# A hand-ordered fused attention and expert kernel: all 766 steps in another order, with engines and buffers assigned anew

## The chip, the cores and the metric

The kernel runs on one core of one Trainium2 chip. The metric is device microseconds (us) of one execution. A core has five engines that run their own instruction streams in order: TensorE (PE in the profile, with its weight loads shown apart as PEld), VectorE (DVE), ScalarE (ACT), GpSimd (POOL) and SyncE (SP). Data moves by DMA, issued here from SyncE, GpSimd and ScalarE. Times are the median of three runs; beside them stands one execution taken by the profiler.

## The reference

Two layers are computed one after the other, for a batch of 4, 8 heads, 768 positions and a head width of 64. The first is sparse attention: each position attends to the keys less than 16 positions away, and to 24 block summaries (the maximum of the keys and the mean of the values over each block of 32). The second is causal attention by four experts of width 64 with top-2 gating on its output.

```python
k_sum = k.reshape(B, H, nb, block, D).max(axis=3)
v_sum = v.reshape(B, H, nb, block, D).mean(axis=3)
...
scores_all = np.concatenate([scores_l_m, scores_s], axis=-1)
...
return np.matmul(a, v_all).astype(np.float32)
...
for e in range(E):
    q = x @ wq[e]
    k = x @ wk[e]
    v = x @ wv[e]
    ...
    ye = a @ v @ wo[e]
```

## The kernel before, in words

The work is cut into 766 steps. A step is a small function that issues one to 48 instructions on one engine, for example "transpose the keys of one pair of heads" or "copy one PSUM result to SBUF". `make_plan` builds the list of steps: for each it gives a name, the engines that may run it, the buffers that it reads and writes, and, for TensorE steps, a mode. The mode tells how the step uses the array: 0 is the whole 128x128 array, 1 is row tiles of 64 (64 rows by 128 columns), 2 is column tiles (64 or 32 columns). Where two successive TensorE steps have different modes, the array changes its shape.

Nothing in the program decides the order at run time. `TABLE` is the order, written out: each entry is the step's index in the plan, a letter for its engine (P TensorE, V VectorE, A ScalarE, G GpSimd, S SyncE) and the slots of the buffers that first come into use in it. `emit` walks the table and issues each step in that order. So the table fixes three things: the order of each engine's own queue, which engine runs a step that several could run, and which physical buffer (slot) a value takes. A step waits, through semaphores, for the steps that write what it reads and for those that last used its slot. The number of slots of each buffer class stands in `SLOTS` (PSUM itself has eight banks).

The names carry the batch b, the pair of heads c (four to a batch) and sometimes a half u or a column group cc. They are used below as follows.

- Startup: `id16`, `idr`, `mt`, `sel`, `pi` build constants; `vone0` to `vone5` write the ones column of the six `vb` slots; `knz`, `kwz`, `vtz`, `v2o`, `zz`, `w1m` clear or fill buffers; `at` is a dummy exponential.
- Loads: `dk` and `dq` bring keys and queries (line 261 and line 266, from GpSimd); `dv` brings the values of one pair (lines 284 to 287, from SyncE); `dvs` brings values for the block sums (line 339); `dw` and `dwv` bring weights (lines 501 and 507).
- Sparse attention, for each pair: `hc` copies the window edges inside the value buffer; `bs` (line 304), `be` and `ds` make the block means of the values by matmul for the first two batches, and `tr` (line 347) by a tree of additions for the others; `tk` and `tq` transpose keys and queries (line 366); `kw`, `rk`, `ksc`, `cq` move the transposed keys, their block maxima and the queries to SBUF; `sc` makes the scores (lines 414 and 420), `ex` the exponential (line 427), `av` the product with the values (line 437); `rc` and `xm` normalise, `tx` transposes (line 463), `hi` and `lo` split the result into two half-precision parts.
- Experts, for each batch: `vp` (lines 554 and 557) makes values and gate logits, `lg`, `v2`, `ga`, `gx`, `gb`, `gc` the gating; `pp` (line 630) makes queries and keys of two experts, `pc` moves them; `sp` (line 654) makes scores, `es` (line 662) the exponential, `dm` (line 667) the causal mask; `aw` (line 678) the product with the values; `r2`, `wv`, `tw`, `ct` scale and transpose; `op` (line 737), `oc` and `od` make, move and store the output.
- `fl` are filler matmuls (line 769), which compute nothing that is used; an `fl` given to ScalarE issues nothing.

Lines 168 and 170 are the helper `copy`: a copy or cast on ScalarE has line 168, one on VectorE or GpSimd has line 170.

Steps of two batches are interleaved: the experts of batch b run among the sparse attention of batch b+1. The last batch's experts run alone.

Of the kernel before, what the change touches and what calls it, by code (L numbers as in the profile page):

```python
# [15 lines left out]
S = 768  # L16
# [43 lines left out]
62,G, 122,P,4.2.2 236,S,4 100,V, 105,P,5.1.1 101,V, 82,P,2.1.1 148,G, 106,A, 81,P, 124,V, 102,P,0.0.0 83,V, 123,A,  # L60
125,G, 107,V, 109,P,6.0 233,G,2 103,A, 84,V, 45,G, 130,P,4.4 144,S,0 110,A, 104,V, 143,S, 269,P,7.0.0 131,A, 141,S,
235,G, 128,P,2.5 271,V, 63,P,6.1 129,A, 145,S,1 108,G, 133,P,0.0.2 270,A, 64,V, 140,S, 132,P, 142,S, 252,P,4.2.2
134,V, 111,P,2.0 135,V, 242,G,0 65,G, 254,V, 113,P,6.1 112,A, 237,G, 85,P,0.1.1 114,A, 86,V, 136,P,2.2.2 272,G, 137,A,
115,P,6.1.0 273,P,5.1 138,V, 150,G, 116,P, 274,A, 87,V, 46,V, 253,A, 238,P,2.0 117,V, 118,V, 246,S,5 277,P,0.2 239,V,
275,P,4.3 278,A, 119,P,6.3.3 256,P,3.2 276,A, 120,V, 241,G, 286,P,2.1.1 303,P,0.0.0 257,A, 194,P,4.0 121,V, 406,S,0
304,A, 244,S,2 255,G, 288,V, 149,G, 196,P,6.1 195,A, 305,V, 240,G, 287,A, 260,P,4.4 147,V, 407,S, 280,P,0.0.1 261,A,
409,S, 247,G, 290,P,3.0 197,A, 307,P,2.1 291,V, 279,P, 308,A, 204,P,4.0 402,S,4 281,V, 213,P,6 152,P,2.0.0 205,A,
282,V, 214,A, 245,G, 258,P,0.5 154,V, 283,P,4.4.4 259,A, 153,V, 408,S, 198,P,6 215,G, 201,P,2 284,V, 146,S, 199,A,
289,G, 248,P,0.1 418,S,0 306,G, 285,V, 401,G,1 202,A, 309,P,6.0 249,V, 210,P,4 310,A, 262,P,2.1.2 211,A, 263,P, 251,G,
165,P,0.2 250,A, 404,S,3 264,V, 265,V, 415,G,0 294,P,6.1 403,G, 166,A, 266,P,4.5.5 292,P,2.2 295,A, 267,V, 158,P,0  # L70
293,A, 400,G,0 151,A, 155,P,6 410,G, 159,V, 268,V, 160,A, 311,P,2.3 157,V, 207,P,4 312,A, 167,P,0.0 156,V, 161,V,6.0
208,A, 163,V, 411,G,0 314,P,2.0.0 162,A, 168,V, 432,P,7.2 313,P, 164,V, 433,A, 169,P,4.1 315,V, 172,P,0 170,A, 316,V,
413,G, 296,P,6.1.1 584,S,0 582,S, 585,S, 449,P,2.0 583,S, 173,A, 181,P,4 203,G, 450,V, 297,P, 412,G, 182,A, 184,P,0
178,P,2 416,S,2 298,V, 299,V, 185,A, 175,P,4 179,A, 209,G, 317,P,0.6.6 183,G, 300,P,6.7.7 174,G, 318,V, 176,A, 206,G,
428,P,2.2.2 200,G, 445,P,3.1.1 171,G, 319,V, 301,A, 177,G, 362,P,4.1 429,A, 414,G,2 447,V, 186,G, 180,G, 302,V,
364,P,0.0 448,A, 576,G,1 446,A, 430,V, 212,G, 586,G, 217,P,0.0.6 363,A, 218,P, 365,V, 431,A, 216,P, 375,P,2.0 219,V,
369,P,4 376,A, 187,P,1.1.0 220,V, 189,P, 587,G,1 370,A, 188,P, 434,P,2.5 190,V, 366,P,6 191,V, 323,P,4.1.1 367,A,
435,A, 436,P,0.4 417,G, 325,V, 420,S,0 453,P,6.3 423,S, 192,P,2.0 324,V, 454,A, 421,S, 320,P,4 193,V, 422,S, 368,G,
437,A, 578,S,5 405,G, 221,P,2.1 322,A, 372,P,6 222,V, 479,P,0.0.0 373,A, 419,G, 462,P,1.2.1 321,V, 381,P,2 223,P,4.0
464,V, 480,A, 577,G,2 335,P,6.2 382,A, 224,V, 463,A, 377,G, 383,G, 590,G,2 326,P,2 336,A, 481,V, 225,S, 371,G, 374,G,  # L80
378,P,4 327,V, 333,P,6.0 328,A, 329,V,1.1 424,G, 331,V, 330,A, 379,A, 229,P,2.2 332,V, 334,A, 451,P,4.0 230,V, 380,G,
226,P,0.4 452,A, 425,G,0 346,P,6.1 227,V, 343,P,4 347,A, 385,P,1.0.2 384,P, 386,P, 344,A, 228,S, 349,P,0 387,V,
604,P,6.1.2 350,A, 599,S,0 345,G, 388,V, 337,P,4 597,S, 427,G, 466,P,7.1 338,A, 606,V, 340,P,0 456,P,2.0.2 341,A,
605,V, 348,G, 455,P, 465,G, 467,A, 482,G, 483,P,4.2 457,V, 438,P,0.1.0 607,G, 458,V, 484,A, 588,G, 439,P, 389,P,6.0
580,S,4 440,V, 352,P,4 468,P,2.2 390,V, 353,A, 351,G, 469,A, 470,P,4.1 441,V, 354,G, 487,P,6.3 339,G, 471,A, 342,G,
621,P,2.2.1 625,P,3.0 591,G,1 488,A, 622,V, 608,P,0.1 594,S,3 579,G, 485,P,4.0 609,A, 355,P,0.1.6 623,V, 356,P, 626,A,
357,P, 426,G, 486,A, 459,P,0.0.0 358,V, 442,P,2.1.1 359,V, 460,A, 489,P,4.0.1 624,G, 443,A, 581,G, 461,V, 490,P,
473,P,6.1.2 444,V, 592,S,0 612,P,0.5 589,G, 491,V, 360,P,2.1 492,V, 613,A, 472,P, 361,V, 493,P,4.2.2 474,V, 629,P,0.4
598,S, 475,V, 494,A, 596,S, 394,P,2.0 630,A, 495,V, 391,P,6.4 395,A, 476,P,0.3.3 392,A, 396,S, 610,P,4.0 477,V,
627,P,2.3 611,A, 393,S, 538,P,6.1 478,V, 231,S, 628,A, 540,P,4.0 539,A, 600,G, 397,P,0.0 541,V, 642,P,2.2 398,A,  # L90
# [12 lines left out]
573,P,4.0 683,V, 706,G, 20,A,3 682,A, 571,A, 724,G, 707,P,1.0.0 684,V, 708,P, 22,A,3 574,A, 572,S, 734,P,6 710,V,
# [798 lines left out]
```

## Time and profile before

| what | us |
|---|---|
| median of 3 runs | 162.57 |
| lowest and highest of them | 161.71, 163.44 |
| the profiled execution's own time | 163.03 |
| its span, from the first to the last instruction | 161.3 |
| TensorE busy in it | 146.8 |
| ScalarE busy | 117.9 |
| VectorE busy | 116.6 |
| GpSimd busy | 111.8 |

The profiled execution is 0.46 us above the median of the runs. The 1.7 us between its span and its own time lie outside the program's instructions. The granted TensorE clock is 1.0 in all stretches. A busy time is the union of an engine's instructions; TensorE's matmuls overlap each other, so its busy share says that it had work, not how fast it went. A row of the timeline gives start, duration, engine, line, operation, output and inputs, shape and count, and in brackets how long the engine had been idle before it and who ended that.

### The profile page before, as it was taken

The page shows a single profiled execution, that of the slowest core. Times are in us where ns is not written, and L with a number is a line of the kernel's source. Part 1 is how long each engine was busy: PE and PEld are TensorE (multiplying, and loading weights), DVE is VectorE, ACT ScalarE, POOL GpSimd, SP SyncE. Part 2 cuts the span into 40 slices and gives each one's busy share as a digit, 9 for nine tenths or more (in the row PEclk, how much of TensorE's full clock was granted, in tenths as well). Part 3 has the DMA queues.
Part 4 walks back from the last instruction along what each step waited for, and adds up shares of the span by engine and source line. Part 5 has one row for each costly group of instructions (what it writes and reads, how often), then busy time and mean ns, then how long its engine had stood idle before and what let it go on. Part 6 is the DMA issues. An engine that isn't in the chain of part 4 may idle for free.

```text
span 161.3 us, 6957 instructions
## 1 busy us (share of the span) xinstructions
PE 146.8 (91%) x2999; PEld 108.0 (67%) x2999; DVE 116.6 (72%) x241; ACT 117.9 (73%) x150; POOL 111.8 (69%) x181
## 2 busy tenths in 40 slices
PE   0249998899999999999999999999999998999997
PEld 0127796786776866688656979666778895476742
DVE  5675488989885577986877887847978578247770
ACT  3032499758998969988978795787867894999540
POOL 6899969777775999969999999629994340135100
DMA  3999999998699995993899749886000000030746
GB/s 27 210 220 212 205 179 227 209 219 163 154 176 207 228 207 135 171 201 53 201 219 221 216 107 161 191 291 254 24 0 4 4 4 0 6 130 0 257 167 230
DMA packets 44158, 24.57 MB, mean 152 GB/s; under 512 B 33120, under 2 KB 40544, under 8 KB 43744
## 3 DMA queue, kind: packets, MB, share of 16 engines
q1 hardware_dynamic: 35280, 16.52, 43.2%
q0 software_dynamic: 7488, 6.29, 26.2%
q10 hardware_dynamic: 1360, 1.32, 2.3%
q8 instruction: 23, 0.38, 1.0%
q14 instruction: 7, 0.06, 0.1%
HBM read 24.13 MB, written 6.29 MB: 189 GB/s over the span
## 4 chain that ended last, share of the span: by engine, by line
PE 65%; POOL 21%; issue 6%; ACT 4%; DVE 3%; POOLq 0%; DVEq 0%; ACTq 0%
PE ps L437 12%; PE ps L630 11%; POOL vb L170 7%; PE ps L554 6%; PE ps L678 6%; PE ps L304 4%; PE ps L366 4%; PE ps L654 4%; PE ps L737 3%; PE ps L463 3%; PE ps L414 3%; POOL vt L347 3%; PE ps L769 3%; POOL a L667 2%; PE ps L420 2%
## 5 line engine op out<-in xcount | busy, mean ns | idle before, releaser
L662 ACT ACTIVATE a<-ps 128x1024 f16<-128x1024 f32 (+1 forms) x48 | 41.8, 918 | 5.2 <-PE ps L654 4.8
L667 POOL TENSOR_SCALAR_AFFINE_SELECT a<-a 128x256 f16<-128x256 f16 x48 | 18.6, 406 | 21.0 <-ACT a L662 20.4
L427 ACT ACTIVATE aT<-ps 120x768 f32<-120x768 f32 x32 | 25.0, 816 | 9.2 <-PE ps L420 9.0
L437 PE MATMUL ps<-vb,aT 120*64 120x65 f32 x768 | 27.3, 224 | 1.2 <-issue 0.6
L437 PEld LDWEIGHTS ps<-vb,aT 120*64 120x64 f32 x768 | 24.4, 138 | 4.3 <-issue 2.1
L170 POOL COPY vb<-vb 32x1408 f32<-32x1408 f32 x16 | 21.9, 1373 | 2.9 <-DMA vb<-in_v_dram 2.1
L630 PE MATMUL ps<-hi,wqk 128*128 128x384 f16 x128 | 23.1, 326 | 0.7 <-ACT ob L168 0.3
L347 POOL TENSOR_TENSOR vt<-vt 120x1024 f32<-120x1024 f32 (+3 forms) x16 | 19.2, 1200 | 6.4 <-issue 4.1
L630 PEld LDWEIGHTS <-wqk 128*128 128x128 f16 x128 | 11.8, 98 | 9.6 <-issue 2.2
L382 DVE TENSOR_REDUCE ks<-ps 128x24 f16<-128x768 f16 x16 | 15.1, 951 | 3.7 <-PE ps L366 3.3
L482 DVE TENSOR_TENSOR lo<-ps,hi 128x768 f16<-128x768 f32 x16 | 15.1, 954 | 1.3 <-ACT hi L168 1.1
L452 DVE TENSOR_TENSOR x<-ps,rec 128x768 f32<-128x768 f32 x16 | 15.3, 956 | 0.5
L366 PE MATMUL ps<-idr,kn 100*64 100x100 f16 x256 | 8.5, 218 | 7.3 <-DMA kn<-in_k_dram 7.3
L654 PE MATMUL ps<-qk,qk 64*128 64x512 f16 (+3 forms) x128 | 14.4, 306 | 0.5 <-ACT qk L168 0.4
L554 PE MATMUL ps<-wvg,hi 128*128 128x264 f16 x96 | 13.8, 275 | 0.1
L170 POOL COPY vb<-vu 24x768 f32<-24x768 f32 x16 | 13.2, 822 | 0.8
L168 ACT COPY kw<-ps 128x1152 f16<-128x1152 f16 x12 | 13.5, 1133 | 0.0
L168 ACT COPY qT<-ps 128x768 f16<-128x768 f16 x12 | 9.5, 806 | 5.3 <-PE ps L366 5.2
L678 PE MATMUL ps<-v,a 128*128 128x65 f16 x336 | 12.3, 193 | 0.2
L366 PEld LDWEIGHTS <-kn 100*64 100x64 f16 x256 | 7.0, 116 | 8.1 <-DVE vb L210 5.7
L678 PEld LDWEIGHTS <-a 128*128 128x128 f16 x336 | 11.0, 97 | 2.1 <-issue 1.0
L737 PE MATMUL ps<-wo,wT 128*128 128x512 f16 (+1 forms) x50 | 11.9, 371 | 0.0
(95 smaller groups left out, 273.8 us busy)
## 6 DMA issues: line engine op xcount, KB each, us to landing
vb<-in_v_dram SPq DMA_DIRECT2D x32, 176.0 KB, 6.1
out_dram<-ob SPq DMA_DIRECT2D x9, 512.0 KB, 3.4
vt<-in_v_dram SPq DMA_DIRECT2D x16, 192.0 KB
kn<-in_k_dram POOLq DMA_DIRECT2D x6, 384.0 KB, 7.5
qn<-in_q_dram POOLq DMA_DIRECT2D x6, 384.0 KB, 7.4
out_dram<-ob ACTq DMA_DIRECT2D x2, 512.0 KB
kn<-in_k_dram POOLq DMA_DIRECT2D x4, 192.0 KB, 5.5
qn<-in_q_dram POOLq DMA_DIRECT2D x4, 192.0 KB, 5.5
```

The costliest lines, as they stand in the source:

```text
L168: nc.scalar.copy(dst, src)
L170: en(e).tensor_copy(dst, src)
L347: en(e).tensor_tensor(y[0:120], x[0:120, 0:w], x[0:120, w:2 * w], AL.add)
L366: nc.tensor.transpose(dst[64 * hp:64 * hp + 64, p * s:p * s + p], src[:, hh + hp, 64 * s:64 * s + 64], idt)
L427: nc.scalar.activation(T["aT"][aT.slot][0:KR], pbank(sc, 2)[0:KR, :, 0:384], AF.Exp, scale=SCALE)
L437: nc.tensor.matmul(pbank(av, 2)[o:o + 64, u, 65 * (2 * (t // 2) + hp):65 * (2 * (t // 2) + hp) + 65], a[0:KR, hp, 64 * t:64 * t + 64], T[" ...
L554: nc.tensor.matmul(p[:, i, 0:264], hi_(ch)[:, cols], T["wvg"][:, ch, :], start=(ch == 0), stop=False, skip_group_check=True)
L630: nc.tensor.matmul(pbank(pp, 2)[:, u, 0:384], T["wqk"][:, cc, ch, j, :], hi_(ch)[:, 384 * u:384 * u + 384], start=(ch == 0), stop=(ch == N ...
L654: nc.tensor.matmul(pbank(sp, 2)[:, ep, c0:c0 + w], T["qk"][qk[1].slot][r, 128 * tj:128 * tj + 128], T["qk"][qk[0].slot][r, n0:n0 + w], sta ...
L662: nc.scalar.activation(a2v(u), pbank(sp, 2)[:, :, 0:ln], AF.Exp, scale=SCALE / (XS * XS))
L667: nc.gpsimd.affine_select(m, m, [[0, 2], [1, 128]], AL.is_ge, 0.0, base=0, channel_multiplier=-1)
L678: nc.tensor.matmul(pbank(av, 2)[:, ep, 65 * ti:65 * ti + 65], a2v(u)[:, ep, o:o + 128], T["v2"][v2.slot][:, tj, 2 * cc + ep, :], start=(tj ...
```

## The change

Only `TABLE` changes: every step is there once, as before, and the functions of the steps and the buffer sizes are the same. The order of each engine's queue, the engine of 61 steps and the slots are new. The order before has 111 changes of array shape between successive TensorE steps, the new one 121. The coarse order is the same (batches and stages follow each other as before); most steps move by a few places.

Among the steps that change engine are: `ds00`, `ds01` and `hc01` from GpSimd to ScalarE, `ds03` and `ds12` from ScalarE to GpSimd; `ksc` five from GpSimd to ScalarE and two the other way; `kw` four from ScalarE to VectorE and one the other way; `cq`, `hi`, `pc`, `v2`, `oc` and `ct` some in each direction; `cvg` from VectorE to ScalarE; eight `fl`.

The first four lines and the last ones, as they were and as they become (the lines between are of the same kind; what the prediction speaks of is given by names below):

```diff
 TABLE = """
-2,G,0 139,A, 41,V,4 6,G, 8,V, 52,S,4 4,G, 7,G, 37,G,0 42,V,5 0,G, 5,G,0 47,S,0 1,A, 36,G, 3,G, 39,V,2 66,S,2 35,G,
-34,V, 59,G,1 58,G,1 71,P,0.0.0 43,G, 88,P,1.1.1 53,G, 90,V, 61,S,5 60,G, 54,P,2.0 72,V, 91,A, 89,A, 48,G, 73,V,
-92,P,3.0 55,V, 57,G, 75,P,4.1 93,A, 232,G,0 49,P,5.1 76,V, 74,A, 56,G, 96,P,6.0 50,V, 94,P,0.1 97,A, 79,P,2.2 67,G,
-95,A, 99,P,6.0.0 40,V,3 77,P,4.3 51,G, 234,S,3 68,P,0.0 78,A, 126,P,1.2 69,V, 80,A, 98,P, 243,G,0 127,A, 44,G, 70,A,
...
-741,P,0.1.2 740,P, 735,A, 711,V, 575,S, 29,P,4 743,V, 712,P,4.0 24,A,6 12,A,6 709,P, 736,G, 744,V, 713,A, 745,P,6.1
-742,P, 746,V, 754,P,4.4 747,V, 714,V, 748,V, 751,P,6.2 755,A, 715,V, 749,P,2 23,P,0 752,V, 756,A, 716,P,4 31,P,1
-717,A, 32,P,0 17,A,1 30,P,1 750,V, 753,A, 757,P,4.6 763,P,5.0 758,A, 760,P,0.1 27,P,1 764,V, 21,P,6 11,A,7 26,A,2
-761,V, 25,A,3 19,P,2 759,S, 765,A, 13,P,7 762,A, 15,A,4 28,A,1 16,A,3 18,A,5 14,P,6 33,P,2 10,P,0
+4,G,0 139,A, 40,V,3 2,G, 8,V, 52,S,3 39,G,2 35,G, 47,S,2 3,G,0 42,V,5 5,G, 58,G,1 6,G, 66,S,5 7,G, 34,V, 37,G,0
+88,P,0.0.0 53,A, 90,V, 60,G, 89,A, 59,G,1 61,S,0 43,G, 91,G, 54,P,1.0 36,G, 92,P,2.0 55,V, 48,G, 71,P,3.1.1 93,A,
+75,P,4.1 57,G, 56,A, 73,V, 94,P,6.0 232,G,2 49,P,5.1 72,V, 95,A, 67,G, 96,P,0.1 76,A, 126,P,2.2 50,V, 148,G, 74,A,
+97,A, 77,P,6.2 127,A, 41,V,4 99,P,4.0.0 78,A, 109,P,3.0 234,S,4 68,P,2.0 51,A, 243,G,1 98,P, 69,V, 44,G, 62,G, 110,A,
...
+682,A, 571,A, 724,G, 733,G, 708,P,0.0.6 684,V, 707,P, 574,A, 572,S, 741,P,1.1.4 710,V, 734,P,0 25,A,2 740,P, 735,A,
+711,V, 575,S, 743,V, 712,P,2.0 12,A,0 26,A,0 20,A,0 709,P, 744,V, 736,G, 713,V, 745,P,0.1 742,P, 11,A,2 746,V, 714,V,
+754,P,2.0 715,V, 747,V, 751,P,0.4 748,V, 755,A, 749,P,6 716,P,4 752,A, 756,S, 717,V, 750,V, 757,P,2.6 753,A, 760,P,3.2
+763,P,4.3 758,A, 23,P,5 761,V, 30,P,6 764,V, 29,P,7 759,A, 17,P,0 765,S, 16,A,1 762,A, 27,A,5 24,A,2 33,A,3 31,A,6
+14,A,7 15,A,4 18,A,1 32,A,1 13,A,1 28,A,1 21,P,1 22,P,2 19,P,3 10,P,4
 """
```

By names, the queues that the prediction follows are these. Before, GpSimd begins `dk000 id16 dk001 idr vone0 w1m dq001 mt dq000 kwz dk011 dq010 sel hc01`, TensorE `tk00 tk01 bs01 tq01 tq00 bs00 sc011`. In the new order GpSimd begins `dk001 dk000 vone2 kwz dq000 dq001 dq010 id16 idr vone0 dq011 dk011 sel ksc01 mt hc00`, TensorE `tk01 bs01 tq01 tk00 tq00 sc010 bs00`, and ScalarE `hc01 kw01 cq01 ds01 ex010 cq00 ksc00`. Ahead of `bs12`, SyncE issued `dv13 dvs200 dv12` and now issues `dv12 dv13`; TensorE's `sp010` and `sp015` stood before `bs12` and now follow it. Around 95 us GpSimd's queue is now `dm102 ds22 ksc30 hc32 hc22 ds30`; `hc22` stood 25 places earlier in it. At the end VectorE's queue is `ct301 ct311 oc33 oc34` and `oc30` is on ScalarE, where before VectorE had `oc30 ct311 oc34 oc33` and `ct301` was on ScalarE; the single filler between `aw310` and `tw300`, and those between `tw311` and `op32`, now follow `op34`.

More of the change, by code (lines that the diff above doesn't have):

```diff
@@ L61 @@
[L61 to L90, printed above, removed]
@@ new lines @@
+136,P,6.2.2 117,V, 273,P,2.1 118,V, 137,A, 307,P,3.2 238,P,4.0 272,A, 138,V, 274,A, 150,G, 308,A, 275,P,0.2 239,V,
+46,G, 119,P,6.3.3 276,A, 244,S,0 277,P,2.3 286,P,5.2.0 120,A, 240,G, 256,P,4.0 287,V, 278,A, 196,P,0.0 255,A, 241,G,
+257,A, 288,V, 194,P,2.1 246,S,2 197,A, 121,V, 289,G, 149,G, 303,P,4.0.2 195,A, 290,P,5.1 304,V, 260,P,0.5 147,A,
+204,P,6.0 408,S,0 279,P,2.0.1 406,S, 261,A, 305,V, 409,S, 280,P, 245,G, 205,A, 407,S, 152,P,0.0.0 402,S,3 281,V,
+282,V, 291,A, 258,P,6.1 154,A, 283,P,4.4.4 259,A, 247,G, 153,V, 201,P,2 284,V, 202,A, 146,S, 306,G, 248,P,0.1 285,V,
@@ new lines @@
+449,P,6.0 432,P,7.1 318,V, 215,G, 450,A, 300,P,2.7.7 403,G, 178,P,0 433,A, 319,V, 445,P,6.1.1 418,S,5 179,A,
+428,P,7.2.0 301,V, 184,P,4 414,G,1 185,A, 175,P,0 302,V, 364,P,4.1 183,G, 176,A, 171,G, 447,V, 180,G, 177,G, 362,P,2.0
+365,A, 430,V, 186,G, 586,G, 446,A, 429,V, 216,P,0.0.0 218,P, 363,A, 188,P,1.1.4 217,P, 369,P,6.0 576,G,0 219,V,
+375,P,2 448,A, 370,A, 189,P, 220,V, 431,G, 587,G,1 187,P, 376,A, 366,P,6 190,V, 323,P,0.1.1 367,A, 191,V, 434,P,2.5
+324,V, 325,V, 192,P,4.0 436,P,6.1 435,A, 412,G, 193,V, 420,S,0 453,P,0.0 423,S, 221,P,2.1 454,A, 422,S, 335,P,4.2
@@ new lines @@
+222,V, 421,S, 437,A, 368,G, 578,S,2 377,G, 405,G, 381,P,0 372,P,2 336,V, 382,A, 462,P,6.0.2 373,A, 479,P,7.2.1 464,V,
+378,P,0 223,P,4.0 379,A, 374,G, 320,P,2 480,A, 224,V, 380,G, 577,G,0 451,P,0.3 321,V, 383,G, 481,V, 225,S, 326,P,4
+452,A, 419,G, 322,V, 463,A, 333,P,0.0 327,V, 371,G, 329,V,7.1 328,A, 424,G, 331,V, 330,A, 229,P,2.2 334,A, 332,V,
+226,P,4.4 230,A, 590,G,1 346,P,0.1 227,V, 343,P,6 347,A, 386,P,1.0.2 425,G,0 384,P, 344,A, 228,S, 385,P, 337,P,4
+387,V, 604,P,0.1.0 338,A, 388,V, 349,P,6 466,P,1.2 350,A, 606,V, 352,P,4 427,G, 456,P,2.0.2 597,S,0 353,A, 467,V,
@@ new lines @@
+444,V, 610,P,0.3 595,G, 493,P,4.2.2 474,V, 611,A, 475,V, 394,P,6.0 494,V, 579,G, 397,P,0.4 395,A, 495,V, 476,P,2.3.3
+591,G,0 396,S, 391,P,6.2 477,A, 398,V, 540,P,4.1 392,A, 478,V, 399,S, 538,P,0.0 393,S, 541,A, 600,G, 627,P,6.0 539,V,
+655,P,2.2.1 628,A, 638,P,3.1.0 656,V, 551,P,4.0 548,P,0 552,A, 589,G, 499,P,6.0.0 657,V, 549,A, 509,P,4.2 500,V,
+601,G,0 639,V, 501,A, 554,P,0 510,A, 545,P,6 640,V, 642,P,2.1 555,A, 502,P,4 643,V, 546,A, 641,G, 496,P,0 553,G,
+504,V, 550,G, 503,V, 581,G, 557,P,2 542,P,6 497,V, 498,V, 558,A, 644,P,4.2 543,A, 615,P,2.0.0 505,V,0.0 507,V, 614,P,
```

37 lines of the change are left out of this document (23 added, 14 removed).

## The prediction

> **What bounds the kernel now.** I read the busy times and the chain of waits of the page first, then the busy time of each engine by stretch.
>
> ```profile
> PE 146.8 (91%) x2999; PEld 108.0 (67%) x2999; DVE 116.6 (72%) x241; ACT 117.9 (73%) x150; POOL 111.8 (69%) x181
> ...
> PE 65%; POOL 21%; issue 6%; ACT 4%; DVE 3%; POOLq 0%; DVEq 0%; ACTq 0%
> ```
>
> ```profile
> core 0: us, PE busy (x) PEld busy (x) DVE busy (x) ACT busy (x) POOL busy (x), PEclk, DMA share, GB/s
> 0.00:9.00 9.00, 1.66 (x32) 1.40 (x32) 4.89 (x20) 1.49 (x2) 7.23 (x29) 1.00 0.82 130
> 9.00:16.00 7.00, 4.81 (x76) 3.40 (x72) 5.20 (x8) 2.58 (x4) 6.69 (x11) 1.00 1.24 214
> 16.00:150.00 134.00, 130.20 (x2794) 97.91 (x2787) 101.20 (x199) 110.36 (x140) 97.43 (x142) 1.00 0.71 144
> 150.00:161.30 11.30, 10.19 (x115) 5.28 (x111) 5.35 (x15) 3.44 (x5) 0.41 (x1) 1.00 0.62 233
> ...
> 9.00:38.00 29.00, 25.38 (x696) 20.97 (x692) 22.91 (x48) 19.58 (x25) 23.99 (x32) 1.00 1.17 207
> 38.00:58.00 20.00, 19.44 (x378) 14.12 (x372) 15.21 (x29) 17.91 (x22) 16.13 (x17) 1.00 0.99 189
> 75.00:101.00 26.00, 25.64 (x599) 19.49 (x598) 20.51 (x40) 21.54 (x29) 24.81 (x37) 1.00 0.87 177
> ```
>
> TensorE has work for 91% of the span and carries 65% of the chain. The rows by stretch show where it has none: it is busy 1.66 of the first 9 us and 4.81 of the next 7, and from 16 to 150 us only 3.8 us of 134 are free. A new order leaves the matmuls as they are. It can win in three ways: the start, those 3.8 us, and the end. It can lose by more changes of array shape and by making another engine late. ScalarE is busy 110.36 of the 134 us, so it is the nearest to being late. GpSimd carries 21% of the chain, and from 75 to 101 us it is busy 24.81 of 26.
>
> **The start.** The first matmuls of the sparse part, `bs01`, are what the start leads to.
>
> ```profile
> 3.80 0.14 POOL L210 MEMSET vb<- 96x24 f32 x1
> ...
> 4.66 0.10 POOL L214 MEMSET vb<- 16x2 f32 x1
> ...
> 4.85 0.72 POOL L266 DMA_DIRECT2D qn<-in_q_dram  x1
> 5.57 0.22 POOL L195 MEMSET mt<- 128x128 f16 x1
> ...
> 6.83 0.37 POOL L199 TENSOR_SCALAR_AFFINE_SELECT mt<-mt 64x96 f16<-64x96 f16 x1
> ...
> 10.28 0.18 POOL L244 TENSOR_SCALAR_AFFINE_SELECT sel<-sel 96x2 f32<-96x2 f32 x1
> 10.52 1.35 POOL L170 COPY vb<-vb 32x1408 f32<-32x1408 f32 x1
> ```
>
> ```profile
> 5.74 0.88 PE L366 MATMUL ps<-idr,kn 100*64 100x100 f16 x16 [5.74 <-DMA kn<-in_k_dram]
> 11.92 1.50 PE L304 MATMUL ps<-vb,sel 96*32 96x128 f32 x22 [0.78 <-POOL vb L170]
> ```
>
> ```profile
> L427 ACT ACTIVATE aT<-ps 120x768 f32<-120x768 f32 x32 | 25.0, 816 | 9.2 <-PE ps L420 9.0
> L168 ACT COPY kw<-ps 128x1152 f16<-128x1152 f16 x12 | 13.5, 1133 | 0.0
> L168 ACT COPY qT<-ps 128x768 f16<-128x768 f16 x12 | 9.5, 806 | 5.3 <-PE ps L366 5.2
> L168 ACT CAST hi<-ps 128x768 f16<-128x768 f32 x9 | 7.0, 805 | 1.7 <-PE ps L463 1.7
> L168 ACT COPY vb<-vs 24x1536 f32<-24x1536 f32 x2 | 2.9, 1471 | 0.1
> ```
>
> `bs01` needs `sel` and `hc01`. Both were on GpSimd, one behind the other: `sel` ends at 10.46, `hc01` takes 1.35, `bs01` starts at 11.92. Now `hc01` is on ScalarE, beside `sel`, at an estimated 1.35 (1471 ns of a copy of 1536 elements, by 1408/1536). GpSimd's queue ahead of `sel` exchanges `mt` (5.57 to 7.20, 1.63) for `vone2` (0.96, by `vone0` from 3.80 to 4.76) and one more query load issued ahead (0.72), 1.68 together; so `sel` still ends at 10.5 and `bs01` starts at about 10.5, 1.4 earlier. Against it, `tk00` (0.88) ran at 5.74 while TensorE had nothing else and now follows `bs01`. Net −0.5; if the values for `hc01` land late, nothing or +0.9. I carry −0.2, but it is not a term of the sum, because a later wait takes it away:
>
> ```profile
> 39.47 0.38 SPq L339 DMA_DIRECT2D vt<-in_v_dram  x1
> ...
> 45.34 1.35 POOL L170 COPY vb<-vb 32x1408 f32<-32x1408 f32 x1 [1.72 <-DMA vb<-in_v_dram]
> 46.16 0.65 PE L654 MATMUL ps<-qk,qk 64*128 64x512 f16 x4
> 46.83 0.77 PEld L304 LDWEIGHTS ps<-vb,sel 96*32 96x32 f32 x26 [0.32 <-ACT aT L427]
> ```
>
> `bs12` starts at 46.83, 0.14 behind `hc12`, which waited 1.72 for its values. The idle 0.32 is put down to the exponential, but `hc12` ended as late: the load is the gate. Its DMA stood in SyncE's queue behind `dvs200` (issue 0.38); now it does not, so the values come about 0.4 earlier and `bs12` can start at about 46.4. Behind it then lie `sp010` and `sp015`, done before it until now. The row at 46.16 (four matmuls of 512 columns in 0.65) prices two matmuls of each at up to 0.33, about 0.15 where they overlap their neighbours; I take +0.3 for both, bounds 0 and 0.65. **Term one: −0.1**, between −0.5 and +0.3; the start's −0.2 would pay nothing, its +0.9 little more than half.
>
> **ScalarE in the first 38 us.** Between 9 us and the first `pp` step the 25 instructions on ScalarE are 10 `ex`, 5 `kw`, 5 `cq`, 2 `hi`, 2 `ksc`, 1 `ds`. The new order puts `hc01` (1.35), `ds` (+1.47), `cq` (+0.81), `hi` (+0.81) there: +4.4, and `at`, which ran before 9 us. By their means the old ones sum to 21.8 and the window has 19.58 busy, since successive instructions overlap; so +4.4 counts as 4.0, and ScalarE would be busy 23.6 of 29, a share of 0.81 against 0.68. From 38 to 58 us it reaches 0.90, from 75 to 101 us 0.83. I take that as possible at no cost: **term two: 0**, but upward it is the largest unknown (rival one). GpSimd gives up what ScalarE takes, and two waits of TensorE on copies should shrink:
>
> ```profile
> 25.64 0.34 PE L414 MATMUL ps<-pi,mt 64*128 64x384 f16 x2 [0.66 <-ACT kw L168]
> 32.37 0.85 PE L437 MATMUL ps<-vb,aT 120*64 120x65 f32 x21 [0.55 <-POOL vb L170]
> ```
>
> Before `bs12` these 1.2 us would only lengthen the wait for the load, so they aren't counted.
>
> **Changes of shape.** The same eight matmuls at two places, once with a change behind them (128 rows to 64) and once without:
>
> ```profile
> 51.12 1.47 PE L630 MATMUL ps<-hi,wqk 128*128 128x384 f16 x8
> 52.53 0.34 PE L414 MATMUL ps<-pi,mt 64*128 64x384 f16 x2
> ...
> 111.04 1.47 PE L630 MATMUL ps<-hi,wqk 128*128 128x384 f16 x8
> 112.35 0.28 PE L554 MATMUL ps<-wvg,hi 128*128 128x264 f16 x1
> ```
>
> The next step starts 1.41 us after them with a change and 1.31 without: 0.10 a change. Of the ten more, six lie before `bs12`, in front of the load's wait; four behind it. **Term three: +0.4**, bounds 0 (where TensorE waits for others anyway) and +1.0 (all ten on the path).
>
> [...]
>
> **75 to 101 us.** GpSimd's queue up to `dm102` loses `hc22`, `ds30` and a `ksc` and so is shorter, where GpSimd is busy 24.81 of 26. But TensorE is free for only 0.36 there. **Term four: −0.2**, bounds −0.36 and 0.
>
> **The end.**
>
> ```profile
> 154.43 1.22 DVE L170 COPY ob<-ps 128x1024 f32<-128x1024 f32 x1 [0.38 <-PE ps L737]
> 155.57 0.28 DVE L170 COPY wT<-ps 128x256 f16<-128x256 f16 x1
> 155.63 1.10 PE L737 MATMUL ps<-wo,wT 128*128 128x512 f16 x6
> ```
>
> The last matmuls, `op32` and after, start at 155.63 as `ct311` (155.57 to 155.85, on VectorE behind `oc30`) delivers. With `oc30` on ScalarE, VectorE is free from 154.43, so `ct311` could come up to 1.1 earlier; what is late next is the transposes `tw311` that it copies, which follow the same `aw` as before, and `ct301` (0.28 again) just ahead of it. I take a quarter. The output DMA follows as before. **Term five: −0.3**, bounds −0.5 and +0.4 (if `oc30`, now in ScalarE's queue, delays its last copies by as much).
>
> **Sum.** −0.1 + 0 + 0.4 − 0.2 − 0.3 = −0.2 against the profiled 163.03, which lies 0.46 above the median; against the median 162.57 that is **162.4**.
>
> **Rivals.**
>
> *ScalarE becomes the bound of the start (slower).* Place: 9 us to the first `pp`. It decides if ScalarE, whose work comes piecewise from TensorE (9.0 of the 9.2 us idle of the `ex` group are waits for scores), can't reach a share of 0.81 so early. If it stays at 0.68, 23.6 us take 34.9, +5.9; halfway, at 0.75, 31.6, +2.6. For it: TensorE's own first tens of us depend on ScalarE's `kw`, `cq` and `ex`. Against it: 0.83 and 0.90 later on. 162.4 + 2.6 = 165.0.
>
> *The new order takes TensorE's waits away (faster).* Half of the 3.8 us free between 16 and 150 us go: 162.4 − 1.9 = 160.5. For it: the waits are on copies of other engines (0.66 and 0.55 above), and 61 steps change engine. Against it: the wait for `bs12` is a load, and 6% of the chain is issue, which no order takes away.
>
> *It only pays its shapes.* None of the gains arrives, all ten changes are on the path: 162.57 + 1.0 = 163.6.
>
> *A new wait at `av220`.*
>
> ```profile
> 101.21 0.92 PE L437 MATMUL ps<-vb,aT 120*64 120x65 f32 x24
> ...
> L437 PE MATMUL ps<-vb,aT x192: 220/222/271, 89.1 to 101.9; 120*64 120x65 f32 x192
> ...
> vb<-in_v_dram SPq DMA_DIRECT2D x32, 176.0 KB, 6.1
> ```
>
> `hc32` now stands in front of `hc22` on GpSimd, and `av220` (101.2 at present) needs `hc22`. `hc32` needs the values of its pair, whose slot is free only after `av210`, in the stretch of `av` that begins at 89.1 and that I put at 91 for its end. 91 + 6.1 + 2 × 1.35 = 99.8: in time by 1.4. A load that takes 3 us more makes it late by 1.6: 164.0. Everything behind `hc32` on GpSimd would wait with it, `ds30` too.
>
> **How the numbers follow.** Forecast 162.4: 0.36. ScalarE's start 165.0: 0.22. Waits gone 160.5: 0.25. Shapes only 163.6: 0.10. `av220` 164.0: 0.07. The range leaves out about a tenth on each side: the lower half of "waits gone" (all 3.8 us would be 158.6), and ScalarE's start beyond its halfway price: 160.3 to 165.2. A difference within 1%, 1.6 us, is about what a measurement of this kernel can tell from none; the limits are 160.9 and 164.2. Faster: most of the waits case with a little of the forecast, 0.27. Slower: ScalarE's start, half of `av220`, and the rest's upper ends (a start at +0.9, shapes at a higher price), 0.30. Within 1%: 0.43.
>
> **What would show it.** Right: `bs01` at about 10.5 with `sel` just before it; ScalarE busy about 23.6 of 29 us from 9 to 38; `bs12` near 46.4 behind a copy that waited for its load; TensorE's idle from 16 to 150 us near 3.5 us; `op32` some 0.3 earlier relative to the last `aw`. Wrong: waits of TensorE on `ex` or `kw` from 16 to 38 us (ScalarE's rival); `bs12` waiting for no load, so that the start counts in full; a wait of `hc32` for values near 97 us; a step between the same matmuls that costs other than 0.10 at a change of shape.

## The result and the profile after

Over 21 runs of each, the median was 162.57 us against 162.64 us before; the ratio of the new order's time to the old was 0.9947, with a 95% interval of 0.9921 to 0.9972. That is 0.5% faster, some 0.9 us (0.4 to 1.3), and less than the 1% that I had called telling. Single runs of the new order lie between 160.39 and 165.76 us, of the old between 161.71 and 165.77. The ratios here go by the runs within 1.5% of their kernel's fastest (12 of these 21 and 18 of the old ones), and the profiled executions of the changed kernel and of head, scal, less, split and best are not among them, so their rows show where the time went in one execution and not what a ratio is made of. The profiled execution of the changed kernel took 162.94 us with a span of 161.2. I read its first 57 us by stretches over several traces.

First the page of the changed kernel, busy time of each engine and the chain; then its busy time by stretch, with the columns of the table before.

```profile
PE 143.5 (89%) x2992; PEld 107.1 (66%) x2992; DVE 116.8 (72%) x236; ACT 119.5 (74%) x152; POOL 109.9 (68%) x184
...
PE 69%; ACT 12%; POOL 5%; issue 4%; DMA 4%; SPq 2%; DVE 2%; POOLq 0%; ACTq 0%; DVEq 0%
```

```profile
0.00:9.00 9.00, 0.88 (x16) 0.81 (x16) 4.84 (x16) 0.58 (x1) 7.27 (x28) 1.00 0.83 131
9.00:16.00 7.00, 5.30 (x90) 4.14 (x94) 3.57 (x7) 5.57 (x6) 5.61 (x15) 1.00 1.28 229
16.00:150.00 134.00, 128.88 (x2795) 97.51 (x2788) 103.54 (x200) 109.96 (x144) 96.59 (x141) 1.00 0.72 143
150.00:161.20 11.20, 8.43 (x105) 4.66 (x101) 4.83 (x16) 3.43 (x4) 0.41 (x1) 1.00 0.63 231
...
9.00:38.00 29.00, 24.08 (x650) 20.11 (x652) 19.89 (x41) 23.18 (x28) 21.34 (x37) 1.00 1.18 209
```

GpSimd has nearly left the chain (21% to 5%), ScalarE has grown in it (4% to 12%) and the output DMA has come into it (4%). ScalarE is busy 23.18 of the 29 us from 9 to 38 where it was 19.58. TensorE's free time from 16 to 150 us grew from 3.8 to 5.1 us in this execution. The rows of its timeline show where 2.1 us of that are:

```profile
30.00 1.26 PE L437 MATMUL ps<-vb,aT 120*64 120x65 f32 x34 [0.88 <-issue]
35.84 0.27 PE L366 MATMUL ps<-id,qn 128*64 128x128 f16 x3 [1.26 <-issue]
```

Both are pauses in the middle of a step: `av030` had done 14 of its 24 matmuls, `tq13` 9 of its 12, and for the instruction behind the pause the profile has no releaser. I counted TensorE's instructions (matmuls, weight loads and the few of its sequencer) in every trace. All pauses of 0.2 us and more between 16 and 150 us for which the profile has no releaser, 28 in the 14 traces of this study, stand behind number 193 of a block of 256: behind 705, 961, 1217, 1473, 1985, 2241 and on. They stand at the same numbers in both orders and in all variants, though other steps stand there, and they last from 0.2 to 3.3 us in one run and are not to be seen in the next. The page counts 23 packets, 0.38 MB in all, on the queue named instruction, 16 KB each, and TensorE's 6,019 instructions are 23.5 times 256: about one packet for every 256 instructions.

The packets' own records go with the pauses. Every one of the 28 pauses ends 1.2 to 2.1 us behind the end of such a packet, the one that follows the crossing of the previous of these places: in the changed kernel packets end at 28.67 and 34.44 us and TensorE goes on at 30.00 and 35.84, in the run best one ends at 26.31 and TensorE goes on at 27.64. Nowhere in the 14 traces is TensorE past such a place less than about 1.2 us behind its packet. A packet takes 0.9 to 2.0 us, but it begins late: a median of 2 us behind the crossing of the previous place, and up to 7.2, between 15 and 45 us, and 0.25 us behind 120 us. All pauses longer than 0.3 us lie before 54 us; in the changed kernel the DMA share is 1.09 from 9 to 54 us and 0.59 from there to 150. No profile names the packet as what ends a pause, and no run took the transfers of the start away, so neither why TensorE stands there nor why a packet begins late is shown.

To see the order itself under these pauses, I cut both orders where exactly the same TensorE steps have been issued in both, and took each stretch's time in every trace that has the one or the other order there. This table is worked out from the starts of the named steps in the traces; "to" gives the step that begins the next stretch in the old and in the new order.

```
stretch, to (old / new)     old order, us (traces)     new order, us (traces)
start to sc001 / tq03       16.58 to 17.49 (8)         16.32 to 19.65 (6)
to tx03 / av020             13.56 to 14.30 (7), 20.02  13.66 to 16.11 (5), 19.44
to bs10 / tq13               3.02 to  3.03 (7)          2.43 to  2.88 (6),  3.02
to sp015 / vp00              9.80 to 10.94 (7)          9.61 to 13.47 (7)
to pp001                    12.17 to 13.77 (5)         11.74 to 12.72 (6)
to vp10 / tw010             18.37 to 18.53 (5)         18.01 to 18.02 (8)
to sp102 / sp105            13.54 (4), 14.71           13.45 (8)
to pp201                    30.56 to 31.25 (5)         30.30 to 31.54 (8)
to aw310                    30.17 to 30.18 (3)         30.21 to 30.22 (6)
to the end                  11.49 to 11.52 (5)         11.49 to 11.51 (5)
```

Behind `pp001` (57 us) most stretches repeat to 0.2 us or better; the one to `pp201` varies by 0.7 us in the old order and by 1.2 in the new, and the run gate has 14.71 in the one before it. By the shortest times the new order is 0.36, 0.09 and about 0.26 faster there and 0.04 slower: 0.7 us over 104 us. Between 31 and 57 us, by the shortest times, it gains 0.6, 0.2 and 0.4. In the second stretch the shortest times are nearly equal (13.56 and 13.66), but five of six traces of the new order take 14.7 to 19.4 us there, and six of eight of the old at most 13.82. The sum of all shortest stretches is 2.0 us in favour of the new order; what was measured is 0.9. But 1.4 of the 2.0 come from the runs warm, scal and less (16.32 in the first row, 9.61 and 9.79 in the fourth), which change fillers or engines at the start; without these three the sum is 0.6. So the table shows gains of the new order in the third row and behind 44 us, and settles neither the rest nor what part the pauses have in the ratio.

### The profile page after: what moved, and what is told of

It reads as the page before. It is cut to its first block, busy times and chain, and to the rows that moved or that the text cites. A ratio compares the mean times of both kernels' runs of the same rounds, so it can differ in the third digit from the quotient of the medians.

```text
span 161.2 us, 6956 instructions
## 1 busy us (share of the span) xinstructions
PE 143.5 (89%) x2992; PEld 107.1 (66%) x2992; DVE 116.8 (72%) x236; ACT 119.5 (74%) x152; POOL 109.9 (68%) x184
## 4 chain that ended last, share of the span: by engine, by line
PE 69%; ACT 12%; POOL 5%; issue 4%; DMA 4%; SPq 2%; DVE 2%; POOLq 0%; ACTq 0%; DVEq 0%
PE ps L437 13%; PE ps L630 12%; PE ps L554 6%; PE ps L678 6%; PE ps L654 6%; PE ps L366 6%; PE ps L737 4%; DMA out_dram<-ob 4%; PE ps L304 4%; PE ps L414 3%; PE ps L463 3%; ACT a L662 3%; PE ps L420 3%; ACT aT L427 2%; ACT kw L168 2%
## 5 line engine op out<-in xcount | busy, mean ns | idle before, releaser
L437 PE MATMUL ps<-vb,aT 120*64 120x65 f32 x768 | 26.5, 224 | 1.3 <-issue 0.9
L170 POOL COPY vb<-vb 32x1408 f32<-32x1408 f32 x15 | 20.1, 1350 | 3.7 <-DMA vb<-in_v_dram 3.1
L654 PE MATMUL ps<-qk,qk 64*128 64x512 f16 (+3 forms) x128 | 14.5, 307 | 0.7 <-ACT qk L168 0.4
L168 ACT COPY ob<-ps 128x1024 f32<-128x1024 f32 (+1 forms) x9 | 8.5, 968 | 6.1 <-PE ps L737 3.9
L170 POOL COPY vb<-vs 24x1536 f32<-24x1536 f32 x6 | 8.7, 1467 | 5.9 <-DVE vs L322 5.8
```

Source lines behind the costliest of these rows:

```text
L170: en(e).tensor_copy(dst, src)
L437: nc.tensor.matmul(pbank(av, 2)[o:o + 64, u, 65 * (2 * (t // 2) + hp):65 * (2 * (t // 2) + hp) + 65], a[0:KR, hp, 64 * t:64 * t + 64], T[" ...
L654: nc.tensor.matmul(pbank(sp, 2)[:, ep, c0:c0 + w], T["qk"][qk[1].slot][r, 128 * tj:128 * tj + 128], T["qk"][qk[0].slot][r, n0:n0 + w], sta ...
```

## The experiments

In all of them the ratio is to runs of the kernel before on the same chip; the interval is the 95% one. The runs come from three chips, so two variants are compared by their ratios alone.

**One part at a time: head, tail, mid.** Up to `bs12` both orders have issued the same TensorE steps but two, `sp010` and `sp015`, which the new order has behind it. So the parts can be exchanged (head keeps both in front of `bs12`, mid has only `sp010` behind it); the buffers were assigned anew where a value crosses the seam.

```diff
 TensorE's queue
-tk00 tk01 bs01 tq01
-...
-tx11 sp010 sp012
+tk01 bs01 tq01 tk00
+...
+tx11 sp015 sp010 sp012
 bs12
 ...
```

> The new order up to the step before bs12, the old order behind it. The whole change measured 0.53% faster, about 0.9 us. Theory of the prediction: bs12 waits for a load of values, so what the start wins is lost there again, and this kernel is within 0.2 us of before. Rival: in the trace of the changed kernel the matmuls run at the short durations (0.34 us for a score's first two) from 16.6 us instead of 19.1; if bs12's wait doesn't take that away, this kernel has most of the gain, 0.6 to 0.9 us faster than before.

Measured 1.0051 (1.0014 to 1.0088): 0.8 us slower. Neither theory had that. In the trace the new steps up to `bs12` have the pauses of the changed kernel at the same two instructions, 1.70 and 1.28 us:

```profile
30.80 1.26 PE L437 MATMUL ps<-vb,aT 120*64 120x65 f32 x34 [1.70 <-issue]
36.66 0.27 PE L366 MATMUL ps<-id,qn 128*64 128x128 f16 x3 [1.28 <-issue]
```

The new order of the first 46 us brings nothing by itself. That the pauses are why it is slower isn't shown: they are read in one execution.

```diff
 TABLE
 ...
 dm310
-aw300 gc3 aw301
-...
-oc30 od31 tw301 ct301 ct311 od30 op32 op34
+aw301 gc3 aw300
+...
+tw301 oc30 od31 ct301 ct311 op32 od30 op33
```

> The old order up to 148 us, the new order for the last 68 steps. Theory of the prediction: op32 comes 0.3 us or more earlier and the end with it, 0.3 us faster. Rival: from 155.3 to 160.2 us the DMA engines are full with the last outputs, the first of which is issued at 154.6 in both kernels, so the matmuls win 0.6 us and the end wins nothing: 0.0, within 0.1 us.

Measured 1.0071 (1.0033 to 1.0109): slower, against both theories, but not by the order. At the seam the copy of the last large outputs had been given a buffer that an earlier output's DMA still had to read:

```profile
155.18 1.93 ACT L168 COPY ob<-ps 128x1024 f32<-128x1024 f32 x2 [3.17 <-DMA out_dram<-ob]
```

In the changed kernel the same copy starts 3.8 us behind `aw310`, here 4.4. The run says nothing of the order, and was made again below.

```diff
 TensorE's queue
 ...
 tx11
-sp010 sp012 bs12 sc130 sp011 av100
-...
+sp012 bs12 sp011 sp010 av101
+...
 aw300 aw301
 ...
```

> The old order up to the step before bs12, the new order from there to 148 us, the old one at the end. Theory of the prediction: four more shape changes cost 0.4 us and the shorter GpSimd queue wins 0.2: 0.2 us slower than before. Rival: the waits of TensorE between 46 and 101 us shrink (it is busy 20.0 of 20 and 26.0 of 26 us in two stretches of the changed kernel, 19.44 and 25.64 before), and this kernel is 0.5 to 0.9 us faster.

Measured 1.0076 (1.0047 to 1.0105). It has the same fault, in the copies of `oc30` and of the last two (waits of 0.91 and 2.77 us for an output's DMA): 13.05 us from `aw310` to the end instead of 11.50. The stretches in front of that are good: 18.01, 13.45 and 30.30 us, where the old order has 18.37, 13.54 and 30.56 at best.

**The same again with the output buffers taken as they come free: tail2 and mid2.** The seam of the first is at 131 us, the others as above.

> The old order up to 131 us and the new order from there, with the output buffers taken in the order in which they come free (in the run named tail, the copy of a last output had to wait for an earlier output's DMA because of the buffer that it was given). Theory from the traces: the end is set by the last outputs' DMAs, so op32 comes 0.5 us earlier and the time is that of before, within 0.2 us; in the trace 11.5 us from the start of aw310 to the end, as in before. Theory of the prediction: 0.3 us faster.

Measured 0.9959 (0.9928 to 0.9991): 0.7 us faster, though its trace shows nothing of it. From `aw310` to the end it takes 11.49 us, before 11.50, and from `aw200` to the end 29.97 against 30.0. `op32` does come earlier, 5.3 us behind `aw310` instead of 5.8. The row of the DMA engines' busy tenths (40 slices of 0.28 us from 150 us on) shows for the changed kernel, which ends in the same order, why that brings nothing. The row of before, over the same stretch, stands below it:

```profile
DMA  9999999993100000000399999999999999700000
...
out_dram<-ob SPq DMA_DIRECT2D x2, 512.0 KB
out_dram<-ob ACTq DMA_DIRECT2D x1, 512.0 KB
```

```profile
DMA  9999999997000000000199999999999989700000
```

From slice 20 (155.6 us) to slice 33 (159.5) the DMA engines are full with the last outputs, in the old order as in the new; what the matmuls now deliver earlier waits behind them. So by the trace the tail's order is worth nothing. The 0.7 us of the runs must come from what this one trace doesn't show, or from chance beyond what the interval allows; which of the two stays open. It is also a measure of how far such small ratios can be trusted here.

> The old order up to the step before bs12, the new one from there to 131 us, then the old one, with the output buffers taken as they come free. Theory from the traces: by the tiles of the matmuls the new order has one change of shape fewer behind bs12, not four more, and its TensorE waits less: from pp000 to op22 96.1 us where the old order takes 96.4, so 0.3 us faster. Theory of the prediction: 0.2 us slower. Rival: all of the 0.9 us by which the changed kernel is faster arises here.

Measured 0.9971 (0.9930 to 1.0012): 0.5 us faster, but a zero is within the interval. The prediction's +0.2 is in it too, at its edge. The stretches are again those of the new order, 18.02 and 13.45, but the one to `pp201` takes 31.54 in this execution, the longest of all.

Together the three parts, head, mid2 and tail2, give +0.51%, −0.29% and −0.41%. That is −0.19% in sum, where the whole change gave −0.53%. Each is known to 0.3 or 0.4% only, so the parts don't contradict the whole, nor do they say which of them it comes from.

**The load in front of `bs12`: gate.**

```diff
 SyncE's queue
-dv13 dvs200 dv12 dvs201
+dv13 dv12 dvs200 dvs201
```

> The kernel before with one step moved: in SyncE's queue the load for the block sums (dvs200) stands behind the value load dv12 instead of in front of it. Theory of the prediction: dv12's values come 0.4 us earlier and bs12, which waits for them, starts 0.4 us earlier: 0.3 to 0.4 us faster. Rival: the load's landing is set by how busy the DMA engines are and not by when it is issued, or bs12 waits as long for something else: 0.0, within 0.15 us.

Measured 0.9958 (0.9914 to 1.0002): 0.7 us faster, with no change just inside the interval. GpSimd's row of `hc12` has it:

```profile
44.24 1.35 POOL L170 COPY vb<-vb 32x1408 f32<-32x1408 f32 x1 [0.85 <-DMA vb<-in_v_dram]
```

It starts 1.1 us earlier than before (45.34) and waits 0.85 instead of 1.72. `bs12` gains nothing by that: it starts at 46.65 instead of 46.83, but the whole trace is earlier by as much, and from `vp00` to `bs12` it is 2.60 us in both, as in all seven traces with that start. What stands right in front of `bs12` is TensorE's own work. The load can hold it up all the same: in tail and mid2 the step waits in its middle, 0.53 and 0.17 us, for GpSimd's copy of the values. So the mechanism that the prediction named happens in some executions and not in the one that it was read from; whether the 0.7 us of the runs is that isn't shown.

**The price of a change of shape: shapes.** Fourteen pairs like these, nothing else:

```diff
 TensorE's queue
-av311 av310 sp205 sp202
+av311 sp205 av310 sp202
-tk32 sp210
+sp210 tk32
```

> The kernel before with 14 pairs of neighbouring TensorE steps exchanged between 63 and 147 us, so that the array changes its shape 138 times instead of 111; the engines and buffers are as before. Theory of the prediction: 0.10 us a change, on the path of a busy TensorE: 2.7 us slower than before. Rival one: the price of a change hides beside the next weight load in most places, 0 to 0.8 us slower. [...]

Measured 1.0253 (1.0195 to 1.0310): 4.1 us slower. Divided among the 27 changes that the run was to add, that is 0.15 us each, but the trace takes the number apart. From `av311` to `sp202`, before and in this run, the two views of the timeline are:

```profile
124.29 1.62 PE L437 MATMUL ps<-vb,aT 120*64 120x65 f32 x48
125.84 0.66 PE L654 MATMUL ps<-qk,qk 64*128 64x128 f16 x8
```

```profile
126.83 0.92 PE L437 MATMUL ps<-vb,aT 120*64 120x65 f32 x24
127.68 0.23 PE L654 MATMUL ps<-qk,qk 64*128 64x128 f16 x2
127.84 0.92 PE L437 MATMUL ps<-vb,aT 120*64 120x65 f32 x24
128.69 0.39 PE L654 MATMUL ps<-qk,qk 64*128 64x512 f16 x2
```

`sp202` starts 1.62 us behind `av311` before and 1.86 here. The first two of the fourteen places overlap and cost 0.25 us together, with a wait of 0.26 for ScalarE between them. Of the others, six cost 0.20 to 0.25 us for two changes, one 0.10; in three (0.52 to 0.95, 2.1 in sum) TensorE waits 0.25 to 0.67 us for ScalarE, whose input the exchange has made late. All fourteen sum to 3.7 us. The last two places cost nothing (−0.01). They showed an error in the count: the step pulled forward there is an `sc` ahead of a `tx`, and the rows have 64*128 for both. The plan's mode of `tx` and `tw` is 0, the whole array, while their matmuls use tiles of 64 rows. By the tiles in the rows the old order has 117 changes and the new one 119, of which 90 and 89 lie behind `bs12`.

The price is 0.10 to 0.12 us a change, in the six places.

**More and less work on ScalarE at the start: scal and less.**

```diff
-hc00,G   ds02,G
+hc00,A   ds02,A
```

> The changed kernel with two more copies, hc00 and ds02 (2.8 us), on ScalarE instead of GpSimd, so ScalarE would be busy about 26 of the 29 us from 9 to 38 us (0.90) against 23.2 measured (0.80). Theory of the prediction: up to 0.90 it costs nothing, so the time is within 0.5 us of the changed kernel's. Rival of the prediction: ScalarE is the bound of this stretch already, and the time grows by 1.5 to 2.8 us.

Measured 1.0099 (1.0059 to 1.0138). Against the changed kernel's 0.9947 that is 1.5%, 2.5 us: the prediction's rival. In its trace TensorE now waits for ScalarE's copy of the keys:

```profile
18.48 0.35 PE L420 MATMUL ps<-qT,kw 64*128 64x64 f16 x12 [0.44 <-ACT kw L168]
...
33.70 2.21 PE L437 MATMUL ps<-vb,aT 120*64 120x65 f32 x34 [2.53 <-issue]
```

That is a wait that the changed kernel hasn't. But it is only 0.44 us, and the two pauses of that execution (1.43 and 2.53 us) are longer than in most traces; how the 2.5 us divide stays open. ScalarE is busy 23.49 of the 29 us there, not the 26 that the run aimed at, so a share of 0.90 was not tried.

```diff
-ds00,A   ds01,A
+ds00,G   ds01,G
```

> The changed kernel with ds00 and ds01 (2.9 us) back on GpSimd, so that ScalarE has about 20 us of work between 9 and 38 us as in the kernel before. Two more copies on ScalarE cost 2.5 us (the run scal). Theory one: ScalarE is the bound of the start in the changed kernel, and this one is 0.5 to 2 us faster than it. Theory two: the new order just fits, the next engine (GpSimd) is as late, and the time is within 0.4 us of the changed kernel's.

Measured 1.0001 (0.9963 to 1.0039), 0.9 us slower than the changed kernel. GpSimd is busy 24.22 of the 29 us then, where the changed kernel has 21.34:

```profile
9.00:38.00 29.00, 23.65 (x570) 19.59 (x572) 18.31 (x39) 18.32 (x23) 24.22 (x39) 0.94 1.14 195
```

So neither theory. The second's reason, that GpSimd is then as late, isn't shown: in this trace TensorE has no wait for GpSimd behind the start. What is measured is that moving copies either way, to ScalarE or from it, costs time.

**Fillers in front: warm.**

```diff
 TensorE's queue
-tk01 bs01 tq01
+fl0 fl1 fl2 tk01 fl3 fl4 bs01 tq01
```

`zz`, which the fillers read, moves from GpSimd to the head of VectorE's queue.

> The changed kernel with five of the fillers that run at its end moved to the front of TensorE's queue (three ahead of tk01, two between tk01 and bs01), where TensorE is free until 10.7 us. Theory from the traces: matmuls run at half speed until 15.8 to 18.4 us, differently from run to run; with work in front, TensorE is at full speed when bs01 starts, the steps from 10.7 to 16 us take about 2 us less, and the kernel is 0.8 to 2 us faster than the changed one. Rival: the steps behind wait for loads and copies instead (tq and hc), and it is within 0.4 us of it.

Measured 0.9997 (0.9963 to 1.0031): 0.8 us worse than without, so nearer to the rival than to the theory. The matmuls are short from `tq01` on (a `tq` takes 0.53 us where it took 0.85), `bs00` starts at 14.5 instead of 15.4 us, and then it is given back:

```profile
16.78 0.34 PE L414 MATMUL ps<-pi,mt 64*128 64x384 f16 x2
17.79 0.35 PE L420 MATMUL ps<-qT,kw 64*128 64x64 f16 x12 [0.68 <-ACT kw L168]
18.50 0.92 PE L437 MATMUL ps<-vb,aT 120*64 120x65 f32 x24 [0.36 <-ACT aT L427]
```

`av010` starts at 20.5 in both. In these two executions the waits of TensorE between 16 and 20 us are for ScalarE: the 0.68 and 0.36 above, and 0.36 in the changed kernel for the same exponential. What costs the 0.8 us isn't shown.

**The last outputs in halves: split.** The edit, in short:

```diff
 def oc(e, ...):
-    copy(e, ob[slot:slot + n], ps[0:n])
+    for j in range(n):
+        copy(e, ob[slot + j], ps[j])
 def od(e, ...):
-    en(e).dma_start(out[i0:i1], ob[slot:slot + i1 - i0])
+    for j in range(i1 - i0):
+        en(e).dma_start(out[i0 + j], ob[slot + j])
```

Only for the last batch, and `od30` is issued from SyncE.

> The changed kernel with the last batch's two large outputs copied and stored in halves (four copies and four DMAs instead of two each, the DMAs of the second from SyncE). Theory from the traces: the last 1.5 MB of output keeps the DMA engines full from 155.3 to 160 us, so what counts is when the first of it is issued; here 153.7 instead of 154.6, and the end comes 0.5 to 0.9 us earlier than the changed kernel's. Rival: the end follows the last small outputs, which are issued at the same time as before: no gain, within 0.2 us.

Measured 0.9898 (0.9855 to 0.9942), 0.5% or 0.8 us faster than the changed kernel and 1.0% faster than before. The trace has it where it was expected: 10.47 us from `aw310` to the end, 11.50 before, and the DMA engines are full from 4.9 us behind `aw310` on, not 5.9.

```profile
DMA  0009999999988000000199999999999989910000
```

(40 slices of 0.28 us from 152.5 us; `aw310` starts at 153.2 in this execution.) This is the fastest kernel of the study.

**Old start, new rest, split outputs: best.**

```diff
 TensorE's queue
 ...
 tx00
-tx03 av020 tq11 av021
-...
+av020 av021 tx03 tq11
+...
```

> The old order up to av020 (31 us), the new order behind it, and the last two large outputs copied and stored in halves as in the run named split. Theory from the traces: TensorE pauses without a wait at every 256th of its instructions here and there, and in the new order the pauses before 36 us are longer (0.9 to 1.7 us at one place, 1.3 to 2.0 at the next) than in the old (0 to 0.4); the new order's gains lie between 31 and 75 us (0.6, 0.2, 0.4 and 0.4 us by stretches without pauses) and the split outputs give 1.0. Together 2.2 to 2.6 us, 1.4 to 1.6% faster than before. Rival: the pauses come with the order from 31 us on (the second of them lies at 36 us in it), and this kernel has what the run named split had, 1.0% faster.

Measured 0.9970 (0.9931 to 1.0010): neither. Behind 57 us its stretches are those of the new order (18.02, 13.45, 30.58, 30.22, and 10.46 at the end), and the stretch `tx03` to `bs10`, 2.43 us in the changed kernel, takes 3.02, so that gain belonged to what stands in front of it. Choosing the old start doesn't get rid of the pauses: this execution has one of 3.33 us at instruction 705, where the changed kernel has none.

```profile
27.64 0.31 PE L366 MATMUL ps<-id,qn 128*64 128x128 f16 x1 [3.33 <-issue]
```

Why it is 0.7% behind split stays open.

## Why the prediction was right, and where it wasn't

Forecast 162.4, measured 162.57 in the median and 0.9 us faster by the ratio, where the sum had −0.2: inside the range and within 1% as the likeliest case said. The sum was small for partly wrong reasons, and that it came near is in part luck: term three is 0.5 us too slow and term five 0.3 too fast, and the two offset each other.

*The start.* `sel` ended at 10.65 and `bs01` started at 10.70 (forecast 10.5 for both), 1.2 us earlier than the main part of it before; `tk00` took 0.87 behind it, as said (0.88).

```profile
10.70 1.92 PE L304 MATMUL ps<-vb,sel 96*32 96x128 f32 x24 [2.16 <-POOL sel L244]
12.56 0.85 PE L366 MATMUL ps<-id,qn 128*64 128x128 f16 x12
13.20 0.87 PE L366 MATMUL ps<-idr,kn 100*64 100x100 f16 x16
```

By `sc001` and `tq03`, where both orders have done the same, the shortest times are 16.89 us in the new order (16.32 with the fillers of warm) and 16.58 in the old. So "pays nothing" holds, but not for the reason named, the wait in front of `bs12`: the gain is gone 30 us earlier, and the run warm shows waits for ScalarE there.

*Term one, the gate (−0.1).* This step failed: in the profile that the prediction read, `bs12` didn't wait for the load. The idle 0.32 is that of the weight load. The matmuls in front of it end at 46.81, and its own begin at once:

```profile
46.83 1.42 PE L304 MATMUL ps<-vb,sel 96*32 96x128 f32 x41
```

In the run gate the load came earlier and `bs12` didn't. In the changed kernel `bs12` waits for nothing either, which the prediction had named as a sign of being wrong: it begins at 47.62, right behind the step in front of it, though `hc13` (45.61 to 46.96) still waited 0.86 for its load.

```profile
45.61 1.35 POOL L170 COPY vb<-vb 32x1408 f32<-32x1408 f32 x1 [0.86 <-DMA vb<-in_v_dram]
```

```profile
47.31 0.38 PE L654 MATMUL ps<-qk,qk 64*128 64x512 f16 x2
47.62 1.53 PE L304 MATMUL ps<-vb,sel 96*32 96x128 f32 x48
```

The stretch around it, from `sp015` or `vp00` to `pp001`, gains 0.4 by the shortest times, the size of the term's lower bound, but not by the load; what it comes from isn't shown. The two `sp` steps, priced at +0.3 for moving behind `bs12`, are TensorE's work on either side of it.

*Term two, ScalarE (0).* Forecast 23.6 busy of 29 us, measured 23.18. It cost nothing that the stretches show. But the room above it was drawn too generously: two more copies on ScalarE were expected within 0.5 us and cost 2.5.

*Term three, changes of shape (+0.4).* This step failed as well. Its price was right (0.10; measured 0.10 to 0.12), its count wrong. It took the plan's modes for the shapes; by the tiles in the rows there is one change fewer behind `bs12`, so the term is −0.1. The higher price that the prediction's chance of slower names is shown by no run; the six places of shapes give 0.10 to 0.12.

*Term four (−0.2).* Measured −0.36 from 57 to 75 us and −0.09 in the next 13.5, close in size but earlier than said, and by the shortest times. The last six `aw` and two `sp` steps in front of `sc200` take 3.65 to 3.80 us in four of five traces of the old order, and their like 3.30 in all eight of the new one. In those four TensorE waited 0.18 to 0.33 us for GpSimd's causal masks, as in this row of tail2:

```profile
68.59 1.09 PE L678 MATMUL ps<-v,a 128*128 128x65 f16 x30 [0.21 <-POOL a L667]
```

That fits GpSimd's shorter queue, at another place. The fifth trace, the profile that the prediction read, has 3.30 and no such wait.

*Term five, the end (−0.3).* This failed too. `op32` did come earlier, by 0.6, but the end is set by the output DMAs, which are full from 155.6 us on; the prediction's "the output DMA follows as before" is the sentence that was wrong. It could have been read in the profile before, whose DMA row from 150 us on has the same full slices. (Of `op32` only the second matmul, at 155.91, had to wait for `ct311`; the first stands behind `ct301`.) Measured 0.0 from `aw310` to the end, and in split, which stores the large outputs in halves, the DMA engines are full from 4.9 us behind `aw310` on instead of 5.9 and the same stretch takes 10.47 instead of 11.50.

*The rivals.* ScalarE's start was a place to be afraid of: two copies more there (scal) cost 2.5 us, though the trace doesn't show that ScalarE is the whole of it. "Waits gone" had 1.9 us and came in part at most: 0.9 was measured. The pauses stand under "issue", of which I said that no order takes it away. What I hadn't seen is that an order may make them longer: at the places 705, 961 and 1217 all six traces of the new start have a pause of 1.2 us or more, and one of eight of the old. Each is one execution, so what that costs in the ratio stays open. "It only pays its shapes" and the late `av220` didn't come: `hc22` was done at 99.56 (forecast 99.8), and `av220` started at 100.36 without a wait.

## What to carry to other kernels

Before calling a wait a gate, look at the idle time of the matmuls and not of the weight loads. Count changes of array shape by the tiles in the trace's rows, not by a label in the program, and price them from a pair of places with and without one. Before pricing an earlier last matmul, look at the last slices of the DMA row: where they were full here, an `op32` earlier by 0.5 us (tail2) left the stretch from `aw310` at 11.49 us, before 11.50, and stores in halves (split) made it 10.47. And where a program is reordered for a per cent, compare stretches between steps that both orders have reached, over several traces; a ratio of whole times under 0.5% may have no cause that a trace shows (the tail2 run is 0.4% faster with nothing in its trace).

## What the runs showed of the hardware

TensorE has pauses of 0.2 to 3.3 us without a releaser in the profile, 28 between 16 and 150 us in the 14 traces, all behind numbers of its own instructions that are 193 more than a multiple of 256. It goes on 1.2 to 2.1 us behind the end of a 16 KB packet of the instruction queue. Behind some of the longer pauses the granted clock is lower: behind those of 1.99 us in split, 2.53 in scal and 3.33 in best the granted clock of the next 6 to 9 us is 0.72, 0.74 and 0.63, and behind those of 0.88 to 1.66 us in the changed kernel and in mid it is 1.00. Behind 1.70 us it is 0.72 in less and 1.00 in head.

A change between array shapes cost 0.10 to 0.12 us where TensorE had no wait beside it (six places of the run shapes, two changes each).

The time at which matmuls become short differs between executions of the same instructions, and the granted clock, 1.00 in all the stretches shown of before and after, doesn't show it. In eight traces whose first 19 us are the same program, matmuls become short between 15.4 and 18.4 us; the first of a score take 0.34 us from 16.1 us on in one and 0.51 at 17.5 in another:

```profile
17.49 0.51 PE L414 MATMUL ps<-pi,mt 64*128 64x384 f16 x2
...
19.15 0.34 PE L414 MATMUL ps<-pi,mt 64*128 64x384 f16 x2
```

```profile
16.13 0.34 PE L414 MATMUL ps<-pi,mt 64*128 64x384 f16 x2
16.30 0.34 PE L420 MATMUL ps<-qT,kw 64*128 64x64 f16 x12
```

The first fence is the kernel before, the second the run tail. What sets that time isn't shown.
